# A list for the order of a segment: the recurrent attention half of a two-part kernel, with its evacuations and streamed weights dealt anew

## The chip, the cores and the metric

The kernel runs on one core of one Trainium2 chip. The metric is the device time of one execution in microseconds; three runs of the kernel before gave 1959.92, 1972.41 and 1975.98 us, and their median, 1972.41 us, is the time before. The profile is of one execution of its own.

## The reference

Two independent attentions, their outputs side by side. Part A is a sliding, dilated attention (2048 rows, 32 heads of 20). Part B, which the change is about, is a recurrence over 64 segments of 32 rows, each with 8 memory rows that the segment before has made:

```python
for s in range(n_seg):                                   # 64
    h = jnp.concatenate([mem, xs], axis=1)               # 8 + 32 rows of 640
    q = jnp.einsum('btd,dhe->bhte', h, Wq)               # 32 heads of 192: 640 x 6144 weights
    k, v = ...                                           # the same with Wk, Wv
    scores = jnp.where(mask, q @ k.T * scale, -1e9)
    o = jnp.einsum('bhqk,bhke->bhqe', softmax(scores), v)
    o = jnp.einsum('bhte,hed->btd', o, Wo)               # 6144 x 640
    mem = o[:, :M, :]                                    # feeds the next segment
    outs.append(o[:, M:, :])
```

So each segment needs all four weight matrices (31 MB in bf16), and its memory rows can't be known before the segment before is done.

## The kernel before

Part A runs first, while part B's resident weights are loaded and the others are copied to a DRAM buffer of plain layout (`copy_streamed`, L331). Then `segment` (L677) runs 64 times and `project_late` (L775) makes the remaining output rows.

*Weights.* Each of Wq, Wk, Wv is cut into 4 groups g (8 heads) of 5 pieces dc (128 of the 640 rows, 1536 columns, 384 KB); Wo is cut into 24 pieces of 320 KB, six per group. `STREAMED` (L285) names the pieces that do not fit and are fetched anew in each segment: 8 of k, 10 of v and 6 of o, 24 in all. `get_unit` (L423) gives a piece to the stage that uses it; for a streamed one `fetch` (L418) issues a DMA on SP into a ring of 7 slots (`wstream`). SP takes its DMAs in the program's order, and each waits until its slot's last reader on TensorE (PE) is done.

*Rows.* HX holds the 32 rows `main` that a segment handles itself (8 of memory, 24 of its own) and 32 rows `ahead`: the last 8 rows of four segments, whose projections are made in advance. `RENEW` says which k and v group has its ahead rows projected in a segment (one of each; `project32` then runs 40 matmuls instead of 20); the ahead rows of q are made at the segment's end (`ql`). Between, the late rows wait in buffers Lb, from which POOL copies them into QT and KT (L508); those of v wait in LV[g].

*A segment's stages*, for each of the four groups g:

- q, k: `project_qk` (L521, matmuls L490) into an accumulator (three PSUM banks in rotation); `evacuate` (L524, L497) copies it to `sb` as bf16; `turn` (T, L500, L503) transposes it on PE; `fill_both` (L530, L508) copies the result to QT or KT, which exist once and are overwritten for each group.
- S: `scores` (L551, L558) on PE; `soft_begin` (L563, L565) masks, `soft_exp` (L570) takes the maximum and subtracts it on VectorE and calls Exp on ScalarE, `soft_end` (L576) sums, inverts and writes P on VectorE. t1, which holds the scores, exists once.
- tp: `turn_p` (L591, L595) transposes P on PE; `spread_p` (L599, L601) writes PT on VectorE.
- v: `values` (L543) projects; `keep_values` (L546, L547, L549) copies to Vst on ScalarE, renewed late rows to LV[g] on VectorE. Vst exists once.
- mix (L606, L614) multiplies PT and the values; `keep_mix` (L620, L622) copies the two results to the halves of OT, then POOL copies the late rows out (L623) and stores them (L624).
- out: `project_out` (L634, L642) adds six Wo pieces' products into Y for groups 0 to 2; `project_last` (L657, L664) does group 3.

`turn_x` (L472) brings the next segment's rows from XS into HX once the last projection has read HX, and `load_x` (L468) fetches XS. `join_begin` (L646, ScalarE) and `join_end` (L652, VectorE) add Y's halves; `close` (L667) adds the last projection, transposes the result and writes the memory rows into HX (L672), on which the next segment's first projection waits; POOL stores the output rows (L674).

*Order.* PE, VectorE, ScalarE and SP keep the order in which the program issues their instructions (`manual_schedule`); only POOL's is left to the scheduler. So the text of `segment` is the order on each engine. On PE it reads: q0 k0 q1 Tq0 Tk0 k1 S0 Tq1 Tk1 q2 k2 v0 S1 tp0 Tq2 Tk2 mix0 v1 S2 out0 tp1 q3 k3 mix1 v2 Tq3 Tk3 tp2 out1 (four pairs) S3 out1 (two pairs) mix2 v3 out2 (four) tp3 out2 (two) mix3 ql last, and the turn of ql.

Of the kernel before, what the change touches and what calls it, by code (L numbers as in the profile page):

```python
# [7 lines left out]
FP32 = mybir.dt.float32  # L8
# [15 lines left out]
def part_a(ctx, tc, A_x, A_wqkv, A_wo, out, ident, emit_loads):  # L24
# [241 lines left out]
    with tc.manual_schedule(engines={mybir.EngineType.PE, mybir.EngineType.DVE, mybir.EngineType.Activation}):  # L266
# [4 lines left out]
        for b in range(-1, n_blk):  # L271
# [17 lines left out]
BLOCKS = 18  # L289
LEAD_IN = 114  # L290
HEAD = 5

# [8 lines left out]
def part_b(ctx, tc, B_x, B_mem0, B_Wq, B_Wk, B_Wv, B_Wo, out, ident, n_seg, pre, nbuf, mid):  # L301
# [193 lines left out]
    def to_sb(p, copy):  # L495
        sb = qk_sb.tile([128, 384], BF16, tag="sb", name="sb")
        copy(sb[:], p[:])  # L497
        return sb

    def turn(sb):  # L500
        pt = bank()[:, 0:384].rearrange("p (c j n) -> p c j n", j=4, n=32)
        for c in range(3):
            nc.tensor.matmul(pt[:, c], lhsT=sb[:, 128 * c:128 * c + 128], rhs=ident, start=True, stop=True)  # L503
        return pt
# [22 lines left out]
    def turn_both(s, m, g, sbs):  # L527
        return [turn(sb) for sb in sbs]

    def fill_both(s, m, g, pts, copy):  # L530
# [12 lines left out]
    def values(s, g):  # L543
        return project32([ahead, main] if renewed(s, "v", g) else [main], "v", g)

    def keep_values(g, ps):  # L546
        S_(Vst[:], ps[-1][:])  # L547
        if len(ps) > 1:
            V_(LV[g][:], ps[0][:])  # L549

    def scores(g):  # L551
        Sps = bank()[:, 0:4 * L].rearrange("p (a n) -> p a n", n=L)
        for outer in range(2):
            for a in range(4):
                for h in range(2):
                    k0, k1, c = (0, 128, 2 * h) if outer else (64 * h, 64 * h + 64, 1)
                    at = L * (4 * c + a)
                    nc.tensor.matmul(Sps[64 * h:64 * h + 64, a, :], lhsT=QT[k0:k1, at:at + 64], rhs=KT[k0:k1, c, a, :],  # L558
                                     start=(outer == 0 and a == 0), stop=(outer == 1 and a == 3),
                                     tile_position=(k0, 64 * h))  # L560
        return Sps

    def soft_begin(Sps):  # L563
        t1 = one.tile([128, 4, L], FP32, tag="t1")
        nc.vector.scalar_tensor_tensor(out=t1[:], in0=Sps, scalar=scale,  # L565
                                       in1=mask[:].unsqueeze(1).to_broadcast([128, 4, L]),
                                       op0=ALU.mult, op1=ALU.add)
        return t1

    def soft_exp(t1):  # L570
        mx = small.tile([128, 4], FP32, tag="mx")
        nc.vector.tensor_reduce(out=mx[:], in_=t1[:], axis=AX.X, op=ALU.max)
        nc.vector.tensor_tensor(t1[:], t1[:], mx[:].unsqueeze(2).to_broadcast([128, 4, L]), op=ALU.subtract)  # L573
# [17 lines left out]
    def turn_p(g):  # L591

        pt = bank()[:, 0:256].rearrange("p (l n) -> p l n", l=2)
        for late in range(2):
            nc.tensor.matmul(pt[:, late, :], lhsT=P[:, late].rearrange("p a n -> p (a n)"), rhs=ident,  # L595
                             start=True, stop=True)
        return pt

    def spread_p(pt):  # L599
        PT = one.tile([128, 4, 2, L], BF16, tag="PT")  # L600
        nc.vector.tensor_tensor(PT[:], pt.rearrange("p l (h n) -> p (l h) n", h=2)[:, :, 0:L].unsqueeze(2)  # L601
                                .to_broadcast([128, 4, 2, L]),
                                own[:].unsqueeze(1).unsqueeze(3).to_broadcast([128, 4, 2, L]), op=ALU.mult)
        return PT

# [70 lines left out]

    def segment(s):  # L677
        last = s + 1 == n_seg
        q0 = project_qk(s, "q", 0)
        q0 = evacuate(q0, V_)  # L680
        k0 = project_qk(s, "k", 0)
        if s == 0:
            fetch_first(len(STREAMED["k"][0]))
        k0 = evacuate(k0, S_)
        q1 = project_qk(s, "q", 1)
        q1 = evacuate(q1, S_)
        q0 = turn_both(s, "q", 0, q0)
        fill_both(s, "q", 0, q0, S_)
        k0 = turn_both(s, "k", 0, k0)
        fill_both(s, "k", 0, k0, V_)  # L690
        k1 = project_qk(s, "k", 1)
        k1 = evacuate(k1, S_)
        t0 = soft_begin(scores(0))
        q1 = turn_both(s, "q", 1, q1)
        fill_both(s, "q", 1, q1, S_)
        soft_exp(t0)
        k1 = turn_both(s, "k", 1, k1)
        fill_both(s, "k", 1, k1, S_)
        soft_end(s, 0, t0)
        q2 = project_qk(s, "q", 2)  # L700
        q2 = evacuate(q2, S_)
        k2 = project_qk(s, "k", 2)
        k2 = evacuate(k2, V_)
        v0 = values(s, 0)
        keep_values(0, v0)
        t1 = soft_begin(scores(1))
        PT = spread_p(turn_p(0))
        q2 = turn_both(s, "q", 2, q2)
        fill_both(s, "q", 2, q2, S_)
        k2 = turn_both(s, "k", 2, k2)  # L710
        fill_both(s, "k", 2, k2, S_)
        soft_exp(t1)
        keep_mix(s, 0, mix(0, PT), (S_, S_))
        v1 = values(s, 1)
        keep_values(1, v1)
        if last:
            load_late((0, 1))
        soft_end(s, 1, t1)
        t2 = soft_begin(scores(2))
        Y = ps_y.tile([128, 320], FP32, tag="y")  # L720
        project_out(Y, 0)
        p1 = turn_p(1)
        soft_exp(t2)
        PT = spread_p(p1)
        q3 = project_qk(s, "q", 3)
        q3 = evacuate(q3, S_)
        k3 = project_qk(s, "k", 3)
        if last:
            load_late((2, 3))
        soft_end(s, 2, t2)  # L730
        k3 = evacuate(k3, V_)
        keep_mix(s, 1, mix(1, PT), (S_, V_))
        v2 = values(s, 2)
        keep_values(2, v2)
        load_x(s + 1)
        q3 = turn_both(s, "q", 3, q3)
        fill_both(s, "q", 3, q3, S_)
        k3 = turn_both(s, "k", 3, k3)
        fill_both(s, "k", 3, k3, V_)
        PT = spread_p(turn_p(2))  # L740
        project_out(Y, 1, range(0, 4))
        t3 = soft_begin(scores(3))
        soft_exp(t3)
        project_out(Y, 1, range(4, 6))
        keep_mix(s, 2, mix(2, PT), (S_, V_))
        soft_end(s, 3, t3)
        v3 = values(s, 3)
        keep_values(3, v3)
        if last:
            load_late((4, 5))  # L750
        project_out(Y, 2, range(0, 4))
        PT = spread_p(turn_p(3))
        turn_x(s + 1)
        project_out(Y, 2, range(4, 6))
        part = join_begin(Y)
        keep_mix(s, 3, mix(3, PT), (S_, V_))
        join_end(Y, part)
        if not last:
            gl = (s + 1) % 4
            ql = project32([ahead], "q", gl)  # L760
            sb = to_sb(ql[0], S_)
        Z = bank()[:, 0:160]
        project_last(Z)
        close(s, Z, part)
        if not last:
            pt = turn(sb)
            keep(late_rows(pt, "q", gl, s + 1), "q", gl, S_)
# [63 lines left out]
    def fetch_first(n):  # L831
        for u in first[:n]:
            fetched[u] = fetch(u)
        del first[:n]
# [80 lines left out]
```

## Time and profile before

| | us |
|---|---|
| median of three runs | 1972.41 |
| the profiled execution's own time | 1969.38 |
| its span, first to last instruction | 1967.4 |
| first close of a segment (L672) | 217.1 |
| last one (of 63) | 1875.6 |
| a segment between, mean of 62 | 26.75 |
| granted TensorE clock, mean | 0.995 |

Busy shares of the page run over the whole span, in which part A takes about the first 177 us, segment 0, with all groups renewed and weights still arriving, some 40, and the end some 60. A segment is read from the timeline between one L672 and the next. PE's waits are listed by what ended them; "issue" means that PE waited for nothing that the profile shows. The ring's pieces are called t, and wcopy_k, wcopy_v and wcopy_o are the DRAM copies that they come from.

### The profile page before, as it was taken

What the parts mean: (1) busy time and instruction counts of PE and PEld (TensorE: products, weight loads), DVE (VectorE), ACT (ScalarE), POOL (GpSimd) and SP (SyncE); (2) the same over time, 40 slices, a digit from 0 to 9 for tenths busy, and PEclk for the clock granted to TensorE, in tenths of its full rate; (3) what the DMA queues carried; (4) which work ended last, traced back from release to release, by engine and by line L of the source; (5) the groups of instructions that cost most, each with busy time, mean ns of one, the idle gap of its engine ahead of it and who ended that gap; (6) DMA issues with size and microseconds to landing.
All of it is one profiled execution on the core that took longest, in us unless ns stands there. A gap on an engine that the chain in (4) does not pass through costs nothing.

```text
span 1967.4 us, 95413 instructions
## 1 busy us (share of the span) xinstructions
PE 1782.9 (91%) x41224; PEld 1133.8 (58%) x41224; DVE 1159.7 (59%) x3404; ACT 817.3 (42%) x2287; POOL 573.1 (29%) x1340
## 2 busy tenths in 40 slices
PE   8898999998899989999999899989998998998888
PEld 5565555555555555555555555555555555555558
DVE  4785666565566555666556566656566565656540
ACT  4453444444344444344444444444444444443420
POOL 3000323333323333333333332333332233332220
PEclk9999999999999999999999999999999999999999
DMA  9928999999999999999999999999999999999991
GB/s 330 307 58 302 314 351 351 355 342 348 328 349 346 343 344 359 342 352 357 347 353 344 344 357 345 358 340 347 351 351 342 340 355 349 351 345 337 337 384 49
DMA packets 286370, 649.51 MB, mean 330 GB/s; under 512 B 61140, under 2 KB 76946, under 8 KB 285948
## 3 DMA queue, kind: packets, MB, share of 16 engines
q1 hardware_dynamic: 267036, 630.01, 90.2%
q0 software_dynamic: 18400, 13.08, 2.1%
q8 instruction: 323, 5.29, 1.1%
q14 instruction: 99, 0.81, 0.1%
q10 hardware_dynamic: 512, 0.33, 0.1%
HBM read 629.10 MB, written 23.24 MB: 332 GB/s over the span
## 4 chain that ended last, share of the span: by engine, by line
PE 69%; DMA 15%; DVE 11%; issue 4%; ACT 1%; SPq 1%; ACTq 0%; DVEq 0%
PE acc L490 37%; DMA t<-wcopy_v 9%; PE Y L642 6%; PE px L614 5%; PE px L558 5%; PE px L503 4%; PE pq L95 3%; PE px L664 3%; DVE PT L601 3%; DMA t<-wcopy_k 2%; DMA t<-wcopy_o 2%; PE px L595 2%; PE px L789 1%; PE po L161 1%; DVE t L565 1%
## 5 line engine op out<-in xcount | busy, mean ns | idle before, releaser
L490 PEld LDWEIGHTS <-HX 128*32 128x32 bf16 x19380 | 480.9, 96 | 395.2 <-issue 98.4
L490 PE MATMUL acc<-t,HX 128*32 128x384 bf16 x5816 | 411.4, 328 | 37.7 <-DMA t<-wcopy_v 17.0
L490 PE MATMUL acc<-wres_q,HX 128*32 128x384 bf16 x6460 | 327.8, 328 | 57.8 <-DVE HX L672 47.8
L623 POOL COPY OL<-OT 128x96 bf16<-128x96 bf16 x256 | 157.9, 617 | 549.6 <-ACT OT L622 505.9
L497 ACT CAST sb<-acc 128x384 bf16<-128x384 f32 x383 | 183.9, 480 | 299.2 <-PE acc L490 281.8
L490 PE MATMUL acc<-wres_k,HX 128*32 128x384 bf16 x3880 | 241.1, 327 | 7.5 <-issue 6.7
L497 DVE CAST sb<-acc 128x384 bf16<-128x384 f32 x263 | 143.4, 555 | 165.8 <-PE acc L490 153.0
L508 POOL COPY QT<-Lb 128x96 bf16<-128x96 bf16 x252 | 70.5, 280 | 514.0 <-PE px L558 370.5
L547 ACT CAST Vst<-acc 128x384 bf16<-128x384 f32 x256 | 122.4, 478 | 228.5 <-PE acc L490 227.2
L490 PE MATMUL acc<-wres_v,HX 128*32 128x384 bf16 x3224 | 203.0, 328 | 5.7 <-issue 5.6
L642 PE MATMUL Y<-wres_o,OT 128*32 128x320 bf16 x3584 | 198.5, 301 | 4.0 <-ACT OT L622 2.3
L574 ACT ACTIVATE t<-t 128x160 f32<-128x160 f32 x256 | 87.2, 341 | 238.1 <-DVE t L573 234.0
L503 PE MATMUL px<-ident,sb 128*128 128x128 bf16 x1938 | 165.5, 221 | 3.2 <-issue 1.4
L624 POOL DMA_DIRECT2D late_o<-OL x256 | 139.4, 544 | 81.5 <-POOL OL L623 53.5
L508 DVE CAST KT<-px 128x384 bf16<-128x384 f32 (+1 forms) x161 | 77.0, 494 | 145.7 <-PE px L503 145.2
L614 PE MATMUL px<-PT,Vst 64*128 64x80 bf16 (+1 forms) x2048 | 130.3, 211 | 29.6 <-DVE PT L601 23.3
L558 PEld LDWEIGHTS <-QT 64*64 64x64 bf16 (+1 forms) x4096 | 105.8, 109 | 85.2 <-issue 72.7
L503 PEld LDWEIGHTS <-sb 128*128 128x128 bf16 x1938 | 112.2, 98 | 55.7 <-issue 42.8
L601 DVE TENSOR_TENSOR PT<-px,own 128x320 bf16<-128x320 f32 x256 | 124.0, 484 | 34.5 <-PE px L595 31.5
L508 ACT CAST QT<-px 128x384 bf16<-128x384 f32 (+1 forms) x260 | 123.9, 478 | 46.7 <-PE px L503 46.7
L622 ACT CAST OT<-px 128x240 bf16<-128x240 f32 x320 | 107.4, 359 | 83.2 <-PE px L614 76.0
L565 DVE SCALAR_TENSOR_TENSOR t<-px,mask 128x160 f32<-128x160 f32 x256 | 82.8, 324 | 97.2 <-PE px L558 88.5
(97 smaller groups left out, 2483.0 us busy)
## 6 DMA issues: line engine op xcount, KB each, us to landing
t<-wcopy_v SPq DMA_DIRECT2D x640, 384.0 KB, 5.8
t<-wcopy_k SPq DMA_DIRECT2D x512, 384.0 KB, 5.8
t<-wcopy_o SPq DMA_DIRECT2D x396, 320.0 KB, 5.4
wres_q<-in_B_Wq_dram SPq DMA_DIRECT2D x20, 384.0 KB, 7.8
late_o<-OL POOLq DMA_DIRECT2D x256, 24.0 KB, 5.5
wres_q<-late_o SPq DMA_DIRECT2D x16, 384.0 KB, 7.5
wres_o<-in_B_Wo_dram SPq DMA_DIRECT2D x18, 320.0 KB, 7.2
wres_k<-in_B_Wk_dram SPq DMA_DIRECT2D x12, 384.0 KB, 7.8
```

Of the source, the lines that this page charges most:

```text
L490: nc.tensor.matmul(ps[n][32 * j:32 * j + 32, :], lhsT=X[:, dc, :], rhs=w[:, 384 * j:384 * j + 384], start=(dc == 0), stop=(dc == 4), tile_ ...
L497: copy(sb[:], p[:])
L503: nc.tensor.matmul(pt[:, c], lhsT=sb[:, 128 * c:128 * c + 128], rhs=ident, start=True, stop=True)
L508: copy(t[:, :, :, n0:n1], src)
L547: S_(Vst[:], ps[-1][:])
L558: nc.tensor.matmul(Sps[64 * h:64 * h + 64, a, :], lhsT=QT[k0:k1, at:at + 64], rhs=KT[k0:k1, c, a, :], start=(outer == 0 and a == 0), stop= ...
L601: nc.vector.tensor_tensor(PT[:], pt.rearrange("p l (h n) -> p (l h) n", h=2)[:, :, 0:L].unsqueeze(2) .to_broadcast([128, 4, 2, L]), own[:] ...
L614: nc.tensor.matmul(ps[r][lo:hi, 2 * L * k:2 * L * k + 2 * L], lhsT=V[64 * r:64 * r + 64, col:col + hi - lo], rhs=PT[64 * r:64 * r + 64, 2 ...
L622: copy(OT[:, 6 * r:6 * r + 6].rearrange("p c n -> p (c n)"), ps[r][:, 0:6 * L])
L623: nc.gpsimd.tensor_copy(OL[:, g % 2].rearrange("p n c -> p c n"), OT[:, :, 32:L])
L624: nc.gpsimd.dma_start(late_o[s // 4][:, g, s % 4], OL[:, g % 2].rearrange("p n c -> p (n c)"))
L642: nc.tensor.matmul(Y[t:t + 32].rearrange("p (b c) -> p b c", b=2), lhsT=OT[:, slot(c), 0:32], rhs=wide(w, r, gv), start=(i == 0), stop=(i ...
```

## The change

1. `segment` becomes a reader of a list of tokens: FIRST for segment 0 (the order of before), ORDER for the others. A token stands for a stage's instructions on all engines that it uses: e = evacuate, T = turn and fill, sb / mx / sub / send = the softmax's parts (Exp goes with sub), ve = keep_values, ot = keep_mix, tx = turn_x.
2. EVACUATE, FILL and HEADS name the engine (S ScalarE, V VectorE) of each evacuation (ahead rows, main rows), each fill and each half of OT. Before: main rows of q0, k2, k3 on V and the others on S, all renewed ahead rows on V; fills of k0, k3 on V, the rest on S; OT's halves SS, SV, SV, SV.
3. STREAMED names other pieces, as many of each matrix.
4. `turn_both` and `fill_both` become one function, and `soft_exp` gives its maximum to `soft_max`; `fetch_first`'s second call, in segment 0, is gone.

```diff
-STREAMED = {"q": ((), (), (), ()), "k": ((0, 1, 4), (2, 4), (1,), (2, 3)), "v": ((0, 1, 4), (0, 2, 4), (3,), (0, 3, 4)),
-            "o": (3, 7, 10, 16, 18, 20)}
+STREAMED = {"q": ((), (), (), ()), "k": ((1, 4), (0, 2), (2, 4), (0, 4)), "v": ((1, 2), (0, 4), (2, 3, 4), (0, 2, 4)),
+            "o": (4, 11, 15, 18, 19, 22)}
+ORDER = """
+    q.0 k.0 e.k0 e.q0 T.q0 q.1 T.k0 e.q1 k.1 S.0 T.q1 sb.0 e.k1 k.2 mx.0 sub.0 e.k2 q.2 send.0 T.k1 e.q2
+    v.0 ve.0 S.1 sb.1 T.k2 tp.0 PT.0 T.q2 v.1 mix.0 mx.1 ve.1 sub.1 S.2 k.3 q.3 ot.0 send.1 out.0.0
+    out.0.1 e.q3 e.k3 sb.2 mx.2 sub.2 tp.1 PT.1 T.k3 v.2 T.q3 mix.1 S.3 ot.1 send.2 tp.2 out.1.0 ve.2
+    sb.3 PT.2 mx.3 out.1.1 sub.3 send.3 mix.2 v.3 ot.2 out.2.0 tp.3 tx ve.3 out.2.1 PT.3 mix.3 ot.3 part
+    ql join last eql close Tql
+"""
+EVACUATE = {"k0": "SS", "k1": "SS", "k2": "SS", "k3": "SV", "q0": "SV", "q1": "SS", "q2": "SV", "q3": "SS"}
+FILL = {"k0": "V", "k1": "S", "k2": "S", "k3": "S", "q0": "V", "q1": "S", "q2": "S", "q3": "S"}
+HEADS = ("VS", "SS", "SS", "SV")
...
-    def evacuate(ps, copy):
-        return [to_sb(p, c) for p, c in zip(ps, [V_, copy][2 - len(ps):])]
+    def evacuate(ps, copies):
+        return [to_sb(p, c) for p, c in zip(ps, copies[2 - len(ps):])]
...
     def segment(s):
         last = s + 1 == n_seg
-        q0 = project_qk(s, "q", 0)
-        q0 = evacuate(q0, V_)
-        k0 = project_qk(s, "k", 0)
...
+        def step(name, *at):
+            g = int(at[0][-1]) if at else None
+            if name in "qkv":
+                project(name, g)
+            elif name == "e":
+                m = at[0][0]
+                got["sb", m, g] = evacuate(got.pop((m, g)), [engine[c] for c in EVACUATE[at[0]]])
+            elif name == "T":
+                m = at[0][0]
+                turn_and_fill(s, m, g, got.pop(("sb", m, g)), engine[FILL[at[0]]])
...
+        for token in (ORDER if s else FIRST).split():
+            step(*token.split("."))
```

On PE the list gives, from segment 1 on: q0 k0 Tq0 q1 Tk0 k1 S0 Tq1 k2 q2 Tk1 v0 S1 Tk2 tp0 Tq2 v1 mix0 S2 k3 q3 out0 tp1 Tk3 v2 Tq3 mix1 S3 tp2 out1 mix2 v3 out2 (four) tp3 out2 (two) mix3 ql last, and the turn of ql. All matmuls, copies and DMAs are as many as before.

More of the change, by code (lines that the diff above doesn't have):

```diff
@@ L289 @@
 BLOCKS = 18
+FIRST = """
+    q.0 e.q0 k.0 e.k0 q.1 e.q1 T.q0 T.k0 k.1 e.k1 S.0 sb.0 T.q1 mx.0 sub.0 T.k1 send.0 q.2 e.q2 k.2 e.k2
+    v.0 ve.0 S.1 sb.1 tp.0 PT.0 T.q2 T.k2 mx.1 sub.1 mix.0 ot.0 v.1 ve.1 send.1 S.2 sb.2 out.0.0 out.0.1
+    tp.1 mx.2 sub.2 PT.1 q.3 e.q3 k.3 send.2 e.k3 mix.1 ot.1 v.2 ve.2 T.q3 T.k3 tp.2 PT.2 out.1.0 S.3
+    sb.3 mx.3 sub.3 out.1.1 mix.2 ot.2 send.3 v.3 ve.3 out.2.0 tp.3 PT.3 tx out.2.1 part mix.3 ot.3 join
+    ql eql last close Tql
+"""
[5 more added lines that the diff above has]
+    ql join last eql close Tql
+"""
+EVACUATE = {"k0": "SS", "k1": "SS", "k2": "SS", "k3": "SV", "q0": "SV", "q1": "SS", "q2": "SV", "q3": "SS"}
+FILL = {"k0": "V", "k1": "S", "k2": "S", "k3": "S", "q0": "V", "q1": "S", "q2": "S", "q3": "S"}
+HEADS = ("VS", "SS", "SS", "SV")
 LEAD_IN = 114
@@ L741, in segment @@
[L741 to L767, printed above, removed]
+        engine = {"S": S_, "V": V_}
+        got = {}
+        def project(m, g):
+            if m == "v":
+                got["v", g] = values(s, g)
+            else:
+                got[m, g] = project_qk(s, m, g)
+                if last and (m, g) == ("k", 3):
+                    load_late((2, 3))
@@ new lines, in step @@
+        def step(name, *at):
[8 more added lines that the diff above has]
+                turn_and_fill(s, m, g, got.pop(("sb", m, g)), engine[FILL[at[0]]])
+            elif name == "S":
+                got["S", g] = scores(g)
+            elif name == "sb":
+                got["t", g] = soft_begin(got.pop(("S", g)))
+            elif name == "mx":
+                got["mx", g] = soft_max(got["t", g])
+            elif name == "sub":
+                soft_exp(got["t", g], got.pop(("mx", g)))
+            elif name == "send":
+                soft_end(s, g, got.pop(("t", g)))
+            elif name == "tp":
+                got["p", g] = turn_p(g)
+            elif name == "PT":
+                got["PT", g] = spread_p(got.pop(("p", g)))
+            elif name == "ve":
+                keep_values(g, got.pop(("v", g)))
+                if g == 2:
+                    load_x(s + 1)
+                elif last and g in (1, 3):
+                    load_late((0, 1) if g == 1 else (4, 5))
+            elif name == "mix":
+                got["mix", g] = mix(g, got.pop(("PT", g)))
+            elif name == "ot":
+                keep_mix(s, g, got.pop(("mix", g)), [engine[c] for c in HEADS[g]])
+            elif name == "out":
+                g, half = int(at[0]), int(at[1])
+                if "Y" not in got:
+                    got["Y"] = ps_y.tile([128, 320], FP32, tag="y", name="Y")
+                project_out(got["Y"], g, range(4 * half, 4 + 2 * half))
+            elif name == "part":
+                got["part"] = join_begin(got["Y"])
+            elif name == "join":
+                join_end(got["Y"], got["part"])
+            elif name == "tx":
+                turn_x(s + 1)
+            elif name == "ql":
+                got["ql"] = None if last else project32([ahead], "q", (s + 1) % 4)
+            elif name == "eql":
+                got["sbl"] = None if last else to_sb(got["ql"][0], S_)
+            elif name == "last":
+                got["Z"] = bank()[:, 0:160]
+                project_last(got["Z"])
+            elif name == "close":
+                close(s, got["Z"], got["part"])
+            elif name == "Tql":
+                if not last:
+                    gl = (s + 1) % 4
+                    keep(late_rows(turn(got["sbl"]), "q", gl, s + 1), "q", gl, S_)
```

68 lines of the change are left out of this document (5 added, 63 removed).

## The prediction

> **What bounds the kernel now.** I read the sums by engine and the slices first, then the steady stretch of part B, then what TensorE (PE) waited for, then one segment instruction by instruction.
>
> ```profile
> PE 1782.9 (91%) x41224; PEld 1133.8 (58%) x41224; DVE 1159.7 (59%) x3404; ACT 817.3 (42%) x2287; POOL 573.1 (29%) x1340
> ...
> DMA  9928999999999999999999999999999999999991
> GB/s 330 307 58 302 314 351 351 355 342 348 328 349 346 343 344 359 342 352 357 347 353 344 344 357 345 358 340 347 351 351 342 340 355 349 351 345 337 337 384 49
> ```
>
> Two things are nearly full at once: PE at 91% and the DMA engines at nine tenths in nearly every slice. The steady stretch (first close of a segment to the last, 62 segments of 26.75 us) says it sharper, in its last two columns (DMA share, GB/s):
>
> ```profile
> 217.00:1876.00 1659.00, 1515.94 (x36340) 945.56 (x36343) 999.59 (x3160) 709.47 (x2053) 529.94 (x1242) 1.00 0.98 348
> ```
>
> PE's own waits there:
>
> ```profile
> PE acc L490 <- DVE HX L672: 47.8, 63, 1.0
> PE acc L490 <- issue: 31.0, 37, 2.1
> PE px L614 <- DVE PT L601: 22.4, 99, 0.3
> PE acc L490 <- DMA t<-wcopy_v: 11.7, 26, 1.7
> PE acc L490 <- DVE sb L497: 5.4, 16, 0.3
> ```
>
> The first is the recurrence at a segment's end; it stays. The third is PE waiting for the spread softmax. I laid out the timeline of the 62 whole segments, taking for each stage the time from its first matmul to that of the next stage. Per segment the smallest times add up to 24.41 us, what the medians have more is 1.10 (waits that come every time), what the means have more is 1.24 (weight pieces and instruction fetch, irregular). 24.41 + 1.10 + 1.24 = 26.75. The 1.10 sits in few places: 0.25 and 0.17 before and in mix 0, 0.27 before mix 3, 0.22 between v 3 and output 2 (for OT), small change elsewhere. Another 0.51 comes in each segment with renewed v 0 (k 2's two evacuations both on VectorE), 0.13 on average and inside the 24.41. Three of these in the timeline (start, length; the first three lines are tp 0, PT and mix 0, the fourth is output 2 waiting for OT, the last two PT and mix 3):
>
> ```profile
> 1026.54 0.29 PE L595 MATMUL px<-ident,P 128*128 128x128 bf16 x2
> ...
> 1026.90 0.48 DVE L601 TENSOR_TENSOR PT<-px,own 128x320 bf16<-128x320 f32 x1
> ...
> 1027.43 0.42 PE L614 MATMUL px<-PT,Vst 64*128 64x80 bf16 x4 [0.27 <-DVE PT L601]
> ...
> 1039.16 0.73 PE L642 MATMUL Y<-wres_o,OT 128*32 128x320 bf16 x16 [0.17 <-ACT OT L622]
> ...
> 1040.18 0.49 DVE L601 TENSOR_TENSOR PT<-px,own 128x320 bf16<-128x320 f32 x1 [0.33 <-PE px L595]
> ...
> 1040.72 0.25 PE L614 MATMUL px<-PT,Vst 64*128 64x80 bf16 x4 [0.20 <-DVE PT L601]
> ```
>
> **The change, part by part (us per segment, no renewal unless said).**
>
> *Longer PE order.* Smallest times by what follows: a projection 0.82 before another projection, 0.92 before any other stage; a turn (T) 0.17 before a turn or tp, 0.26 before others; S 0.47, mix 0.44; an output stage of six pairs 0.93, cut in two by a score 0.66 + 0.39. Before, 7 of the 12 projections are followed by another shape, now 9 (+0.20); turns now stand alone seven times (1.67 becomes 1.99, +0.32); tp 1 before a turn saves 0.09, output 1 in one piece 0.12. Sum +0.31. The Trainium skill's "TensorEngine Tiling (Array Packing)", Key Properties, says that changing the tiling mode drains the engine; that speaks against this order, and the 0.92 against 0.82 agrees.
>
> *Waits that go.* Between tp 0 and mix 0 now stand a turn and v 1 (0.26 + 0.92), and PT needs 0.36 to its start, 0.49, 0.05 = 0.90: the 0.25 + 0.17 go. S 3 moves ahead of output 1, so softmax 3's Exp is done before mix 2 ends and OT 2 is copied about 0.2 before output 2 asks: 0.22 goes. q 2 between k 2 and v 0 covers k 2's evacuations: 0.13 goes. Small ones 0.14.
>
> *Waits that come.* T q3 now stands two stages ahead of S 3, which reads it. From a turn's first matmul to its fill's start 0.43 to 0.44, fill 0.48, to PE 0.05:
>
> ```profile
> 1023.07 0.53 PE L503 MATMUL px<-ident,sb 128*128 128x128 bf16 x6
> ...
> 1023.50 0.48 ACT L508 CAST QT<-px 128x384 bf16<-128x384 f32 x1 [0.30 <-PE px L503]
> ```
>
> That is 0.97 against a cover of 0.26 + 0.44: a new wait of 0.27. Behind S 3 everything on PE moves with it. If ScalarE were still at k 3's fill it would be 0.75, if its start were 0.16 earlier, 0.1; k 3's fill starts about 1.2 earlier, so I take 0.27. Mix 3 keeps its wait: tp 3 to PT to mix 3 is 0.90, cover 0.21 + 0.39: 0.30 as now. turn_x now stands before PT 3 on VectorE: 0.38 + 0.18 behind softmax 3's end. It waits for the last v 3 matmul and for XS; if it slipped behind tp 3 it would add up to 0.56. Chain of softmax 3 after S 3 (0.11, four steps of 0.36, 0.35 + 0.21 + 0.39, PT 2 between) ends 0.1 to 0.3 ahead of tp 3, so I take 0. In segments with renewed k 1, q 2 waits 0.24 for an accumulator that ScalarE now empties: 0.06. Others 0.05. Sum 0.68.
>
> *Evacuations.* ScalarE gains about 0.8 (second halves of OT 1 and 2 at 0.36, the renewed k rows at 0.48, less OT 0's first half), VectorE loses as much. ScalarE is busy 709.47 / 62 = 11.4 of 26.75: no price beyond the waits above. join now comes after OT 3 on ScalarE: part (2 x 0.29) and join (2 x 0.31) end 0.2 before the last projection does. Cost nothing as long as that 0.2 holds.
>
> *Queues.* SP issues the same 24 pieces a segment (18 of 384 KB, 6 of 320 KB) in the order of their use; XS still follows v 2's pieces, sixteen pieces in, past the previous segment's stores. POOL does the same copies and stores, each waiting for OT or a score that comes within 1 us of where it was. Segment 0 keeps its order; project_late has other pieces streamed, as many: 0 +-3 us in all.
>
> *Pieces.* With the slots laid end to end, the time from the release of a ring slot to the use of its next piece was 5.5 to 8.8 (shortest: v 3's last piece), and will be 5.0 to 9.0; landing takes 5.8 (part 6 of the page). v 3's 5.5 costs 0.10 on average today, so 5.0 for two pieces (output 2's, the last one of project_last) costs between 0 and 1.6; I take nothing, nearest to that row.
>
> *Sum for PE:* 1.23 of waits go to 0.68, the order is 0.31 longer: -0.24, in 63 segments -15 us.
>
> *How much of it reaches the end.* DMA is at 0.98. Segments by renewal (four kinds) have usual PE sums of 25.41, 25.16, 25.73, 25.59, a spread of 0.57; their mean lengths are 26.81, 26.65, 26.80, 26.74, a spread of 0.16. So transfers even out most of what PE saves. On the other hand slices reach 359 GB/s and one segment took 25.0. Between a quarter and all, I take a half: -0.12 x 63 = -8 us. The profiled execution took 1969.4 (span 1967.4 and 2.0 around it), so 1961.8; the median shown is 3.0 above that execution: **1965**.
>
> **Rivals.**
> *Faster in full:* PE's 0.24 all counts, and the pieces, now mostly in pairs two us apart, take a third off the 1.24 of irregular waits (0.41): 0.65 x 63 = 41, 1931. For it: the best segments have almost no irregular wait. Against: the 0.98. Over 1% from 0.31 a segment.
> *Transfers pace it alone:* no change, 1972 (0.16 of 0.57 says nearly that). The Trainium skill's "DMA: Bandwidth & Descriptors", Bandwidth, gives about 358 GB/s from HBM for a core; an estimate from it for a segment's 348 x 26.75 = 9.3 MB is 26.0 us, which would leave 0.77 at most; the slices of 359 and 384 here are above it.
> *Slower, by the late pieces:* output 2's piece and the last one have 5.0 us from slot to use, against 0.3 for the issue and 5.8 to land. Each would be 1.05 late; with the DMA backlog one pays for part of the other, 1.6 in every second segment: (0.8 - 0.24) x 63 = 35, 2007. It decides from 0.55 a segment. Against: v 3's 5.5 today.
>
> **Chances.** A measurement of this kernel tells about 1% from no change (its three runs span 0.8%). Half of PE's gain 0.40 (1965, own range 1950 to 1980, 0.03 of it over 1% faster); in full 0.26; no change 0.11; late pieces 0.23. Faster 0.26 + 0.03 = 0.29, slower 0.23, the rest 0.48. A third of each outer case left out (0.09 + 0.08) gives 1925 to 2012.
>
> **What would show it.** PE waiting for PT about 0.3 x 63 instead of 99 waits, all at mix 3; no wait for OT at output 2; a new wait of S 3 (L573 of the changed kernel) for ScalarE's fill, some 0.27 x 63 = 17 us, put down to PE's weight load; DMA share 0.98 or more at about 350 GB/s; segments of about 26.6. I am wrong if PE's waits for t in output 2 or project_last exceed 0.5 a segment, if PT 3 stands behind turn_x, or if the DMA share falls below 0.97 with the time.

## The result, and the profile after

| | before | after |
|---|---|---|
| median of 11 runs each, same chip, us | 1975.98 | 1952.96 |
| their range | 1959.92 to 1981.97 | 1946.30 to 1960.26 |
| ratio, 95% interval | | 0.9889 (0.9864 to 0.9915) |
| the profiled execution, us | 1969.38 | 1954.89 |
| segment, mean of 62 | 26.75 | 26.55 |

1.1% faster, 22 us by the ratio and 23 by the medians; between the two profiled executions it is 14.5 us, since the one of before lay in the lower half of its runs. Of the 14.3 us between the two spans, 12.6 lie in the 62 segments, 0.5 before them and 1.2 behind them. So 0.20 us a segment by the profiles, about 0.35 by the ratio of all runs (22 / 63).

The page of the changed kernel, sums by engine and the last two rows of the slices:

```profile
PE 1786.8 (91%) x41224; PEld 1129.4 (58%) x41224; DVE 1094.8 (56%) x3206; ACT 870.7 (45%) x2485; POOL 571.0 (29%) x1340
...
DMA  9928899999999999999999999999999999999991
GB/s 329 311 59 292 309 343 349 351 350 361 340 354 353 329 352 352 353 363 338 361 363 344 332 350 347 353 343 338 357 345 352 355 347 362 354 353 354 357 385 60
```

VectorE gave 65 us, ScalarE took 53. The steady stretch, last columns clock, DMA share and GB/s:

```profile
217.00:1862.00 1645.00, 1518.20 (x36332) 939.59 (x36324) 938.79 (x2972) 757.24 (x2231) 526.29 (x1240) 0.99 0.98 350
```

PE is busy as long as before (1518 against 1516) in a stretch that is 14 us shorter: what went is idle time. A segment moves 350 x 26.55 = 9.3 MB, as before. PE's waits in that stretch:

```profile
PE acc L507 <- DVE HX L690: 47.5, 62, 0.9
PE px L632 <- DVE PT L619: 13.8, 59, 0.8
PE px L573 <- ACT QT L525: 13.6, 62, 0.5
PE acc L507 <- issue: 10.5, 20, 1.5
PE Y L660 <- issue: 8.5, 9, 1.9
PE acc L507 <- DMA t<-wcopy_v: 8.4, 20, 1.1
PE px L632 <- issue: 7.0, 7, 1.8
PE px L682 <- DMA t<-wcopy_o: 3.7, 6, 1.2
...
PE Y L660 <- DMA t<-wcopy_o: 2.5, 4, 1.4
```

The wait for PT comes 59 times and no longer 99: mix 0's is gone, mix 3's stays. S 3 (L573) waits once a segment for T q3's fill, 0.21 as the view counts it. The waits for VectorE's evacuations (5.4 us before) are gone. One segment of PE's timeline (start, length) shows T q3, the first line of mix 1, S 3, and then the first two lines of mix 3:

```profile
1028.69 0.34 PE L520 MATMUL px<-ident,sb 128*128 128x128 bf16 x3
1028.96 0.24 PE L632 MATMUL px<-PT,Vst 64*128 64x80 bf16 x4
...
1029.69 0.54 PE L573 MATMUL px<-KT,QT 64*64 64x40 bf16 x16 [0.21 <-ACT QT L525]
...
1034.09 0.23 PE L632 MATMUL px<-PT,Vst 64*128 64x80 bf16 x3 [0.20 <-DVE PT L619]
1035.81 0.21 PE L632 MATMUL px<-PT,Vst 64*128 64x80 bf16 x1 [1.49 <-issue]
```

From T q3's first matmul to S 3's it is 1.00; the fill in ScalarE's timeline starts 0.38 after T q3's first matmul and takes 0.48:

```profile
1029.07 0.48 ACT L525 CAST QT<-px 128x384 bf16<-128x384 f32 x1 [0.38 <-PE px L520]
```

The last PE line is another kind of stall: 1.49 us in the middle of a mix, between two matmuls of the same form on the same operands. VectorE's timeline shows turn_x (two lines) ahead of PT 3, and that it did not hold it: tp 3 starts at 1033.22, PT 3 0.33 later, the usual distance (median 0.32). In 13 of the 62 segments PT 3 starts 0.42 to 0.54 after tp 3, all of them with renewed v 3: there it stands behind the copy of v 3's late rows on VectorE, which costs 0.03 on average.

```profile
1032.99 0.36 DVE L483 STREAM_TRANSPOSE HX<-XS 128x160 bf16<-128x160 bf16 x1
1033.38 0.17 DVE L494 COPY HX<-HX 128x40 bf16<-128x40 bf16 x1
1033.55 0.49 DVE L619 TENSOR_TENSOR PT<-px,own 128x320 bf16<-128x320 f32 x1
```

**A table for all kernels.** Every step from one matmul's start to the next is sorted by where it falls. At the *first matmul of a stage* lie the waits for other engines, the shape changes and the recurrence. At *pieces*: the first matmuls on a streamed piece, what they take beyond the same place of a kernel that streams nothing (experiment 5 below). *Inside*: all other matmuls, likewise less that kernel's. What is left, 17.09 in the new order and 16.96 in the old one (which has one stage boundary more), is PE's own pace inside stages. Microseconds per segment, from the profiled executions:

| kernel | own | first of stage | pieces | inside | segment |
|---|---|---|---|---|---|
| before | 16.96 | 7.89 | 0.53 | 1.37 | 26.75 |
| after | 17.09 | 7.96 | 0.52 | 0.98 | 26.55 |
| 1, after with the old pieces | 17.09 | 8.02 | 0.76 | 0.92 | 26.79 |
| 2, after with the old order | 16.96 | 8.38 | 0.67 | 1.19 | 27.20 |
| 3, after with the old engines | 17.09 | 8.90 | 0.51 | 0.79 | 27.28 |
| 6, before with the new pieces | 16.96 | 7.89 | 1.10 | 1.15 | 27.10 |
| 10, before with the new engines | 16.96 | 8.39 | 0.29 | 1.26 | 26.91 |
| 11, before with the new order | 17.09 | 8.81 | 0.84 | 1.07 | 27.82 |
| 4, after, no Wo pieces | 17.09 | 7.96 | -0.02 | 0.91 | 25.94 |
| 5, after, no pieces at all | 17.09 | 7.99 | 0.00 | 0.09 | 25.17 |
| 7, after, T q3 early | 17.09 | 7.54 | 0.97 | 1.10 | 26.70 |
| 8, 7 with ql split | 16.92 | 7.63 | 0.94 | 1.00 | 26.49 |
| 9, 8 with other pieces | 16.92 | 7.64 | 0.53 | 1.26 | 26.36 |

In the old order, about 0.22 of "inside" and 0.13 of "pieces" are waits for other engines that fall there (mix 0's second part, two of 0.04, and v 0's accumulator).

### The profile page after: what moved, and what is told of

The parts are those of the page before. It is cut to its first block, busy times and chain, and to the rows that moved or that the text cites. A ratio compares the mean times of both kernels' runs of the same rounds, so it can differ in the third digit from the quotient of the medians.

```text
span 1953.1 us, 95447 instructions
## 1 busy us (share of the span) xinstructions
PE 1786.8 (91%) x41224; PEld 1129.4 (58%) x41224; DVE 1094.8 (56%) x3206; ACT 870.7 (45%) x2485; POOL 571.0 (29%) x1340
## 4 chain that ended last, share of the span: by engine, by line
PE 71%; DMA 14%; DVE 8%; issue 3%; ACT 2%; SPq 0%; ACTq 0%; POOL 0%; POOLq 0%; DVEq 0%
PE acc L507 40%; DMA t<-wcopy_o 8%; PE px L520 6%; PE px L573 5%; PE Y L660 4%; DMA t<-wcopy_v 4%; PE px L632 3%; PE pq L95 3%; PE px L682 3%; PE px L613 2%; DVE PT L619 1%; PE px L790 1%; PE po L161 1%; DVE Vst L483 1%; DVE XS L687 1%
## 5 line engine op out<-in xcount | busy, mean ns | idle before, releaser
L507 PEld LDWEIGHTS <-HX 128*32 128x32 bf16 x19380 | 468.1, 96 | 358.6 <-DVE HX L690 59.5
L514 ACT CAST sb<-acc 128x384 bf16<-128x384 f32 x454 | 211.2, 480 | 304.9 <-PE acc L507 293.9
L520 PE MATMUL px<-ident,sb 128*128 128x128 bf16 x1938 | 205.6, 222 | 4.0 <-issue 2.7
L660 PE MATMUL Y<-wres_o,OT 128*32 128x320 bf16 x3840 | 188.4, 301 | 8.5 <-issue 7.3
L640 ACT CAST OT<-px 128x240 bf16<-128x240 f32 x384 | 125.0, 359 | 114.5 <-PE px L632 112.4
L525 ACT CAST QT<-px 128x384 bf16<-128x384 f32 (+1 forms) x195 | 93.4, 481 | 164.5 <-PE px L520 164.5
L514 DVE CAST sb<-acc 128x384 bf16<-128x384 f32 x192 | 106.5, 555 | 102.1 <-PE acc L507 86.8
L660 PEld LDWEIGHTS <-OT 128*32 128x32 bf16 x4608 | 116.3, 96 | 65.6 <-issue 19.7
L573 PE MATMUL px<-KT,QT 64*64 64x40 bf16 (+1 forms) x4096 | 138.3, 189 | 14.3 <-ACT QT L525 13.9
L573 PEld LDWEIGHTS <-QT 64*64 64x64 bf16 (+1 forms) x4096 | 108.0, 109 | 70.4 <-issue 61.8
L632 PE MATMUL px<-PT,Vst 64*128 64x80 bf16 (+1 forms) x2048 | 122.5, 212 | 18.0 <-DVE PT L619 14.2
```

The source lines that it names most:

```text
L507: nc.tensor.matmul(ps[n][32 * j:32 * j + 32, :], lhsT=X[:, dc, :], rhs=w[:, 384 * j:384 * j + 384], start=(dc == 0), stop=(dc == 4), tile_ ...
L525: copy(t[:, :, :, n0:n1], src)
L632: nc.tensor.matmul(ps[r][lo:hi, 2 * L * k:2 * L * k + 2 * L], lhsT=V[64 * r:64 * r + 64, col:col + hi - lo], rhs=PT[64 * r:64 * r + 64, 2 ...
L640: copy(OT[:, 6 * r:6 * r + 6].rearrange("p c n -> p (c n)"), ps[r][:, 0:6 * L])
L660: nc.tensor.matmul(Y[t:t + 32].rearrange("p (b c) -> p b c", b=2), lhsT=OT[:, slot(c), 0:32], rhs=wide(w, r, gv), start=(i == 0), stop=(i ...
```

## The experiments

Ratios are to the kernel before in the same comparison, with their 95% intervals. PE's waits of experiments 1, 5, 6, 7 and 12 are taken from 217 to 1850 us of the span, and those of 10 to 1885; the steady stretches end between 1773 (5) and 1899 (6). One theory was that the new order carries the gain and that the engines and the pieces are there to serve it; the rivals were that one of the parts alone makes it, or that the transfers set the time whatever the order.

### One part taken back: 1, 2, 3

**1**, the pieces:

```diff
-STREAMED = {"q": ((), (), (), ()), "k": ((1, 4), (0, 2), (2, 4), (0, 4)), "v": ((1, 2), (0, 4), (2, 3, 4), (0, 2, 4)),
-            "o": (4, 11, 15, 18, 19, 22)}
+STREAMED = {"q": ((), (), (), ()), "k": ((0, 1, 4), (2, 4), (1,), (2, 3)), "v": ((0, 1, 4), (0, 2, 4), (3,), (0, 3, 4)),
+            "o": (3, 7, 10, 16, 18, 20)}
```

> The changed kernel with the streamed pieces of before. If the order on TensorE made the gain (theory), the time stays at the changed kernel's, ratio to before 0.985 to 0.993 (about 1953 us against 1976). If the new pieces made it (rival), at least half is given back: ratio 0.994 or more.

Measured: 1981.16 us, ratio 1.0048 (1.0015 to 1.0082): the gain is gone, as the rival said. Its waits for pieces:

```profile
PE acc L507 <- DMA t<-wcopy_k: 20.4, 39, 1.5
...
PE acc L507 <- DMA t<-wcopy_v: 10.1, 24, 0.8
```

After has 0.3 us of the first. k 3 now runs before q 3 and 4.0 us after the release of its piece's slot (the usual stage times laid end to end, release of the slot's last reader to first use), where landing takes 5.5 to 5.8 us from issue (part 6 of the page). Not renewed, the stage takes 1.22 in the median and not 0.82; the mean cost at k 3's pieces is 0.39, at v 1's 0.19. The order of after with the pieces of before would not have been faster.

**2**, the order (segments 1 to 63 run in FIRST as segment 0 does):

```diff
-        for token in (ORDER if s else FIRST).split():
+        for token in FIRST.split():
```

> The changed kernel with the list of segment 0 (the order of before) for all segments; new engines for the evacuations and new pieces stay. Theory: TensorE's usual waits come back to about 25.5 us a segment and the ratio to 0.996 to 1.004. Rival (engines or pieces made the gain): ratio below 0.992.

Measured: 1997.44 us, 1.0123 (1.0076 to 1.0170), above the 0.996 to 1.004 of the theory. In the table it has 0.42 more than after at the first matmuls of stages, 0.15 more at pieces and 0.21 more inside.

**3**, the engines:

```diff
-EVACUATE = {"k0": "SS", "k1": "SS", "k2": "SS", "k3": "SV", "q0": "SV", "q1": "SS", "q2": "SV", "q3": "SS"}
-FILL = {"k0": "V", "k1": "S", "k2": "S", "k3": "S", "q0": "V", "q1": "S", "q2": "S", "q3": "S"}
-HEADS = ("VS", "SS", "SS", "SV")
+EVACUATE = {"k0": "VS", "k1": "VS", "k2": "VV", "k3": "VV", "q0": "VV", "q1": "VS", "q2": "VS", "q3": "VS"}
+FILL = {"k0": "V", "k1": "S", "k2": "S", "k3": "V", "q0": "S", "q1": "S", "q2": "S", "q3": "S"}
+HEADS = ("SS", "SV", "SV", "SV")
```

> The changed kernel with the evacuations, fills and halves of OT on the engines of before. Theory (the order made the gain, the engines only keep its covers): TensorE's usual waits rise by 0 to 0.3 us a segment, ratio 0.987 to 0.997. Rival (the engines made the gain): ratio 0.997 or more.

Measured: 2004.92 us, 1.0173 (1.0129 to 1.0218), far outside the 0.987 to 0.997 of the theory. More than all of what it loses against after lies in the first matmuls of stages (8.90 against 7.96 us a segment). One segment of its VectorE, and then of its PE (S 3 and tp 2), shows the larger half:

```profile
1025.53 0.41 DVE L640 CAST OT<-px 128x240 bf16<-128x240 f32 x1 [0.96 <-PE px L632]
1025.86 0.31 DVE L596 TENSOR_REDUCE sm<-t 128x4 f32<-128x160 f32 x1
1026.20 0.18 DVE L597 RECIPROCAL sm<-sm 128x4 f32<-128x4 f32 x1
1026.41 0.58 DVE L606 TENSOR_TENSOR P<-t,sm 128x128 bf16<-128x128 f32 x2
```

```profile
1025.60 0.54 PE L573 MATMUL px<-KT,QT 64*64 64x40 bf16 x16 [0.21 <-ACT QT L525]
1026.89 0.40 PE L613 MATMUL px<-ident,P 128*128 128x128 bf16 x2 [0.75 <-DVE P L606]
```

The list issues ot.1 ahead of send.2. With OT 1's second half on VectorE, VectorE stands 0.96 waiting for mix 1, and softmax 2's sum, reciprocal and P stand behind it although they are ready; tp 2 then waits 0.75 here, and in 61 of the 62 segments (42.3 us in all). HEADS "SS" for group 1 takes that copy off VectorE; that is what the token order needs from the table of engines. Another loss is renewed k 0 with the turn that follows, 0.27 on average: both evacuations of the old deal end later, and T q0 waits for VectorE's `sb`. A third is output 2, which waits 11.7 us in all for the half of OT that VectorE copies.

### One part alone: 6, 10, 11

Each is the kernel before with one of the three. 10 has the new EVACUATE, FILL and HEADS: it is after with the edits of 1 and 2 together. 11 has the new ORDER: it is after with the edits of 1 and 3 together. 6 has the new STREAMED:

```diff
-STREAMED = {"q": ((), (), (), ()), "k": ((0, 1, 4), (2, 4), (1,), (2, 3)), "v": ((0, 1, 4), (0, 2, 4), (3,), (0, 3, 4)),
-            "o": (3, 7, 10, 16, 18, 20)}
+STREAMED = {"q": ((), (), (), ()), "k": ((1, 4), (0, 2), (2, 4), (0, 4)), "v": ((1, 2), (0, 4), (2, 3, 4), (0, 2, 4)),
+            "o": (4, 11, 15, 18, 19, 22)}
```

> The kernel before with nothing changed but the streamed pieces. Theory now (the pieces are fitted to the order, since the changed kernel with the old ones lost all its gain): no gain or a loss, ratio 0.999 to 1.012, with TensorE waiting for v 2's three pieces. Rival (the new pieces are better in any order): ratio 0.993 or less.

> The kernel before with the new engines for evacuations, fills and halves of OT alone (old order, old pieces). With the new pieces as well it was at 1.012, of which some 0.013 is what the new pieces alone cost in the old order. Theory (engines are fitted to the order too): usual times 25.6 to 25.9, ratio 1.000 to 1.008. Rival (the new engines are better by themselves): ratio 0.996 or less.

> The kernel before with the new order alone (old engines, old pieces). With new pieces it was at 1.017, by waits for evacuations (k 0 when renewed, S 3, OT 2: usual times 26.5). The old pieces come 4.0 us after their slots in k 3 in this order. Theory: usual times 26.4 to 26.9, ratio 1.015 to 1.035. Rival (old pieces suit the old engines' slower pace): ratio under 1.010.

Measured: 6, 1993.88 us, 1.0129 (1.0089 to 1.0168); 10, 1979.56 us, 1.0056 (1.0025 to 1.0087); 11, 2032.80 us, 1.0327 (1.0285 to 1.0369). None of the three gains alone, and no two of them do (1 is order with engines, 2 engines with pieces, 3 order with pieces). With before and after these are all eight combinations, and only all three parts together gain. What each lacks can be read from the waits. Kernel 6:

```profile
PE acc L490 <- DMA t<-wcopy_v: 30.8, 48, 2.2
...
PE Y L642 <- DMA t<-wcopy_o: 9.6, 13, 1.4
PE px L664 <- DMA t<-wcopy_o: 5.2, 11, 1.3
```

45.6 us for v and o pieces to 1850 us, against 14.7 in before's whole steady stretch: the pieces are spaced for another order. Kernel 10:

```profile
PE px L632 <- DVE PT L619: 22.9, 101, 0.3
...
PE px L573 <- ACT KT L525: 15.3, 58, 0.8
```

A score waits for k 3's fill, now on ScalarE, in 58 segments, and mix 0's wait for PT is still there. Kernel 11 has both faults of 1 and 3 (in its whole steady stretch 28.7 us for k pieces and 38.6 us of tp 2 for P).

### No weight traffic: 4, 5

Both are after with resident weights in place of streamed ones, so that this part of the computation is changed: in 4 the six Wo pieces, in 5 all 24. All matmuls stay.

The edit of 4, in get_unit (STAND_IN names a resident piece of the same group for each of the six):

```diff
+        if STAND_IN and u[0] == "o" and streamed(u):
+            return res["o", STAND_IN[u[1]], 0]
```

and that of 5 (stand_in gives the group's first resident piece):

```diff
+        if streamed(u):
+            return stand_in(u)
```

> The changed kernel without the six streamed Wo pieces: a resident piece stands in for each, so 18 pieces a segment are fetched instead of 24 and those products are of other weights; the matmuls are as many. Theory (transfers near their limit keep back part of what TensorE saves, 1.48 us of irregular waits a segment): DMA share falls to about 0.8, the irregular waits to under 0.5, the segment to about 25.4 us, some 65 us less: ratio 0.95 to 0.965. Rival (the irregular waits are instruction fetch and do not depend on the weights' traffic): segment 26.2 or more, ratio 0.98 or more.

> The changed kernel without any streamed piece: in segments a resident piece of the same matrix and group stands in for each of the 24, so the products are partly of other weights and the ring is idle; matmuls and instructions are as many. Without 6 of them TensorE still waited 0.43 us a segment for nothing that the profile shows (instruction fetch, by the spacing of about 128 matmuls), and 0.02 for pieces. Theory (those fetches are late because the DMA engines are busy with weights): irregular waits under 0.25, segment 25.1 to 25.3, ratio to before 0.945 to 0.953. Rival (they are late whatever the traffic): irregular waits 0.7 or more, segment 25.7 or more, ratio 0.963 or more.

Measured: 4, 1907.70 us, 0.9672 (0.9621 to 0.9723), DMA share 0.83. It is slower than I expected, 25.94 a segment and not 25.4: the waits for pieces fell to nearly nothing, but the stalls inside stages stayed (0.91 against 0.98). 5, 1858.09 us, 0.9444 (0.9415 to 0.9474). Its steady stretch, and all of PE's waits from 217 us to 1850 (the last two lines lie behind the stretch):

```profile
213.00:1773.00 1560.00, 1479.72 (x36332) 925.47 (x36332) 936.49 (x2972) 756.33 (x2231) 525.66 (x1240) 1.00 0.04 10
```

```profile
PE acc L513 <- DVE HX L696: 49.4, 62, 1.1
PE px L638 <- DVE PT L625: 15.6, 63, 0.4
PE px L579 <- ACT QT L531: 13.3, 62, 0.2
PE px L638 <- issue: 0.6, 1, 0.6
PE px L688 <- ACT OT L646: 0.5, 1, 0.5
```

Three waits are left in a segment: the recurrence, mix 3's, S 3's. So the new order's own pace on PE is 25.17, and 1.38 of after's 26.55 come from the weight traffic, the waits put down to "issue" (29 us in after's steady stretch, none in this one) among them.

### Less PE time: 7, 8, 9, 12

**7** takes away S 3's wait by turning q 3 one stage earlier, ahead of v 2; **8** also does the first of ql's five steps ahead of mix 3, to cover its wait; **9** also picks the pieces anew, so that the shortest time from a slot's release to its use is 5.46 us and no longer 4.33 (after: 4.77).

In all three:

```diff
-    out.0.1 e.q3 e.k3 sb.2 mx.2 sub.2 tp.1 PT.1 T.k3 v.2 T.q3 mix.1 S.3 ot.1 send.2 tp.2 out.1.0 ve.2
+    out.0.1 e.q3 e.k3 sb.2 mx.2 sub.2 tp.1 PT.1 T.k3 T.q3 v.2 mix.1 S.3 ot.1 send.2 tp.2 out.1.0 ve.2
```

In 8 and 9 also (the step ql then takes a part of its five steps; that code is left out here):

```diff
-    sb.3 PT.2 mx.3 out.1.1 sub.3 send.3 mix.2 v.3 ot.2 out.2.0 tp.3 tx ve.3 out.2.1 PT.3 mix.3 ot.3 part
-    ql join last eql close Tql
+    sb.3 PT.2 mx.3 out.1.1 sub.3 send.3 mix.2 v.3 ot.2 out.2.0 tp.3 tx ve.3 out.2.1 ql.0 PT.3 mix.3 ot.3 part
+    ql.1 join last eql close Tql
```

In 9 also:

```diff
-STREAMED = {"q": ((), (), (), ()), "k": ((1, 4), (0, 2), (2, 4), (0, 4)), "v": ((1, 2), (0, 4), (2, 3, 4), (0, 2, 4)),
-            "o": (4, 11, 15, 18, 19, 22)}
+STREAMED = {"q": ((), (), (), ()), "k": ((0, 1, 3), (0, 1), (0, 3), (0, 4)), "v": ((1, 3, 4), (4,), (0, 3, 4), (1, 4)),
+            "o": (0, 11, 16, 17, 20, 23)}
```

> The changed kernel with the turn of q 3 right after that of k 3, ahead of v 2: the fill that S 3 waits for (0.29 us a segment) gets v 2's 0.92 as cover, and one shape switch (0.08) goes. Theory (a saving on TensorE that comes in every segment reaches the end by about a half): usual times fall by 0.37, the segment by 0.15 to 0.25, ratio to before 0.977 to 0.985. Rival (transfers and fetches pace it): segment within 0.05 of the changed kernel's, ratio 0.986 to 0.991. Rival (all of it comes through): ratio 0.977 or less.

> The same, and the first of ql's five steps (0.17 us) stands between the last part of output 2 and mix 3, so that PT 3 is nearer to done when mix 3 asks (it waits 0.26 us there); OT 3's copies keep 0.66 as cover. Theory (half comes through): another 0.05 to 0.1 us a segment, ratio 0.002 to 0.003 below the run with the turn alone. Rivals: nothing (paced by transfers), or a loss, if the pieces of project_last now come too early for their slots.

> The run with the early turn of q 3 and the split ql, with other streamed pieces (as many of each matrix), picked so that the shortest time from a ring slot's release to the use of its next piece, on the usual stage times laid end to end, is 5.5 us; it is 4.3 with the pieces of the changed kernel, which have regular waits there (v 3, output 2, project_last). Theory (what the two shorter covers saved was lost to pieces that came too early for their slots): the regular waits in v 3 and output 2 go, usual times fall to about 24.7, the segment to 26.0 to 26.3, ratio to before 0.972 to 0.984. Rival (the average transfer rate paces the segment, whatever the spacing): segment within 0.1 of 26.5, ratio 0.986 or more.

Measured: 7, 1956.19 us, 0.9916 (0.9891 to 0.9941); 8, 1947.69 us, 0.9896 (0.9855 to 0.9937); 9, 1947.53 us, 0.9902 (0.9869 to 0.9935). The intervals hold after's ratio: none of them can be told from it, though each takes PE waits away. For 7 the expected 0.977 to 0.985 was missed. The table says where the time went. 7 saves 0.42 at the first matmuls of stages and pays 0.45 at the pieces. Its waits:

```profile
PE acc L507 <- DMA t<-wcopy_v: 18.3, 42, 1.4
...
PE px L682 <- DMA t<-wcopy_o: 8.9, 21, 1.8
...
PE Y L660 <- DMA t<-wcopy_o: 4.9, 9, 1.2
```

32.1 us (to 1850 us) where after has 14.6, with S 3's wait gone: v 3 (1.03 in the median, 0.82 in after) and output 2 (0.89, 0.75) now ask for their pieces sooner than the slots allow. 9 mends that (pieces back to 0.53, though 0.26 of it is now at v 0, whose pieces are not those with the shortest time) with own and first of stage together at 24.56 against after's 25.05, but then the stalls inside stages are 0.28 more. The steady stretch of 9:

```profile
217.00:1852.00 1635.00, 1505.45 (x36335) 929.50 (x36336) 938.82 (x2975) 754.33 (x2236) 531.43 (x1241) 1.00 0.99 353
```

I had expected 0.972 to 0.984 of it and missed.

**12** asks how much the transfers leave when PE is far ahead. It leaves out steps dc 1 to 3 of every q projection, 60 of about 586 matmuls of a segment (this part of the sum is not computed), and keeps every transfer.

```diff
-        for dc in range(5)[part]:
+        for dc in (0, 4) if m == "q" else range(5)[part]:
```

> The changed kernel with three of the five steps of each q projection left out (4 groups and ql, 60 matmuls a segment, all of resident weights); all transfers stay. TensorE's usual times fall by 5 x 3/5 x 0.82 = 2.46 us to 22.6 a segment. Theory (the transfers have a pace of their own, near 26 us a segment, and the changed kernel is close to it): the segment falls by no more than 0.7, to 25.8 to 26.5, DMA share 0.99 or more, ratio to before 0.965 to 0.987. Rival (half of what TensorE saves still comes through): 25.3 or less, ratio 0.948 or less.

Measured: 1892.90 us, 0.9645 (0.9583 to 0.9707), segment 25.34:

```profile
218.00:1789.00 1571.00, 1406.23 (x32612) 842.74 (x32612) 936.58 (x2975) 754.26 (x2237) 526.79 (x1241) 0.99 1.00 367
```

PE's pace fell by 60 x 0.041 = 2.46, the segment by 1.21. The line of v pieces in PE's waits, and the rate in slices of 47 us:

```profile
PE acc L507 <- DMA t<-wcopy_v: 46.0, 91, 2.0
```

```profile
GB/s 326 326 74 221 314 374 367 372 374 377 359 377 372 375 358 347 370 368 348 369 363 368 375 352 371 374 357 361 385 365 367 364 376 371 355 376 364 367 374 45
```

The DMA share is 1.00 and PE now stands for pieces, so the transfers hold it up here; but the slots are still released by PE, and single slices reach 385. So 25.3 is the most that the transfers need in a segment, not a measured floor. It is below the 26 that I had expected, and within 0.2 of PE's own 25.17. By the time alone the rival fits about as well: 1.21 of 2.46 is a half, and it asked for 25.3 or less. What speaks against a fixed half are experiments 7 to 9.

## Why the prediction was right, and where not

The time, 1952.96, lies 12 us below the forecast of 1965 and inside the range. The forecast was a gain of 8 us from 1972.41; measured were 22 from 1975.98. "Faster" had the smaller chance (0.29) than "same" (0.48), and it came out at the border between the two.

*PE's sum, -0.24.* It held. By position (own, first of stage, and the engine waits inside: 0.22 + 0.13 before, none after) PE goes from 25.20 to 25.05, -0.15. Counted by medians of stages, as the prediction did, and with the regular waits at pieces taken out, it goes from 25.42 to 25.09, -0.33 (25.51 less 0.09 at v 3's piece; 25.07 less 0.09 at output 2's piece, and 0.11 more for two waits that come in one kind of segment only, below). The forecast lies between the two counts. Its terms:

- S 3's new wait: 0.27 forecast; S 3 with mix 1 is longer by 0.29. The place and the cause are right. That the size is right is luck: the fill starts 0.38 after the turn and not 0.43, but S 3 starts 0.14 after the fill's end (1029.55 to 1029.69 in the lines above, and in the median) and not 0.05, and the two nearly cancel. Why it is 0.14 is not shown.
- Mix 3's wait stays: forecast as before plus 0.03, measured 0.03 less. The turns, with the wait ahead of mix 0: forecast +0.07 (0.32 - 0.25), measured +0.05. Output 1 and the tp stages: -0.21 and some small waits, measured -0.26. All right.
- Accumulators: q 2 in segments with renewed k 1 waits 0.20 (forecast 0.24). Not forecast: q 1 waits 0.22 in those with renewed k 0. Each is 0.05 on average.
- "7 of the 12 projections are followed by another shape, now 9 (+0.20)" was wrong: it is still 7. q 3 and v 3 end in an output stage, and those take 0.81 and 0.82. Both have the tile form 128\*32 (the profile's lines), so nothing changes. The 0.92 of v 3 in before was a wait for OT that never fell below 0.1. I had counted by the name of the stage. The Trainium skill's "TensorEngine Tiling (Array Packing)", Key Properties, says it the right way: changing the *mode* drains the engine, not going to another tile. The same slip hid 0.10 of mix 0, which now stands before S 2 (64\*64 behind 64\*64: 0.34, not 0.44).
- OT's wait at output 2 goes, but only 0.13 of the 0.22 was that wait; the rest stood at v 3's piece. These misses nearly cancel.

*Evacuations at no price:* right for the kernel as changed; VectorE's and ScalarE's other work hides them. Experiments 3, 10 and 11 show that this holds only together with the order: the same order with the old deal costs 0.94 a segment, the new deal in the old order 0.50. The join's margin of 0.2 did not hold: VectorE's half of it ends 0.09 before the close in the median (0.73 in before). The close then starts 0.08 after the last matmul where it was 0.05, so the price was only some 0.02.

*"I take nothing" for the pieces:* about right in size, within its 0 to 1.6. Pieces cost 0.53 before (0.13 of it the accumulator) and 0.52 after, so +0.12. The places are those named: output 2's piece 0.14, the last stage's 0.10; and v 2 and v 3, which I had not named. Shortest time from slot to use is 4.77, forecast 5.0. The rival of late pieces (0.8 a segment) did not come; experiments 1 and 6 show it where pieces and order do not fit. Its sum took 5.8 us to land, the row of the k and v pieces; both pieces that it named are of Wo, whose row has 5.4 in before.

*"I take a half":* this is the step that was mis-sized, on weak grounds. By the profiles 0.20 of 0.15 to 0.33 reached the end, by the ratio of all runs about 0.35; so most of it or all. The argument was that transfers at a DMA share of 0.98 even out what PE saves. Its row, mean lengths that differ by 0.16 where usual sums differ by 0.57, did not show that: each mean is of 15 or 16 segments that spread by 0.79, so its standard error (the scatter to expect of such a mean) is 0.15 to 0.25. Experiment 12 shows that 0.98 was not full: with PE ahead the same bytes flow in 25.3 a segment. Experiments 7 to 9 show the other side: 0.4 to 0.5 more off PE brought nothing that can be measured, by the pieces' slots (7, 8) or by more stalls inside stages (9). No fixed share describes both.

*The rival "transfers alone pace it"* (no change, 0.11) and with it the estimate of 26.0 from the Trainium skill's "DMA: Bandwidth & Descriptors", Bandwidth, fall with experiment 12: 367 GB/s over 1571 us is above the 358 it was worked out from. The Trainium skill's "HBM Reference", Specifications (TRN2), says that 358 is each core's share when both of a pair stream and that one alone gets more; the trace agrees as far as 367.

*What remains open.* Inside stages the stalls fell from 1.15 (1.37 less the engine waits) to 0.98, which is 0.17 of the net 0.20. Across the other kernels that stream all 24 pieces they lie between 0.79 and 1.26 in one profiled execution each, and I can name no edit that sets them, so this part may be chance. Counted as waits for "issue" of over 0.15 us, they are 40 in after and 50 in before, a difference no larger than the chance scatter of such counts (the root of 90 is 9). So what of the gain between the two profiles is the order's, and what is fewer stalls in one execution, stays open. It was not tried whether the kernel before without streaming has 25.2 or 25.4 of its own pace, which would settle PE's sum.

In one picture: PE alone needs 25.17, the transfers alone at most 25.3. Coupled by seven slots, they take 26.55. No change tried here gained without both fewer waits on PE and pieces that fall where the order can use them, and after is the only one of the eight combinations in which both fit.

## What to carry to other kernels

Where two resources are nearly full, measure each one's own pace by taking the other away (no streaming; less compute at all the transfers) before reasoning about what share of a gain comes through. When an order of stages changes, work out anew for each prefetched piece the time from its slot's release to its use, and for each in-order engine which copy stands ahead of which chain; here each of order, engines and pieces cost 0.6 to 3.3% without the other two. And count a shape change by the tile form in the profile's line, not by the stage's name.

## What the runs showed of the hardware that I had not expected

A DMA share of 0.98 at 350 GB/s was no ceiling: experiment 12 ran 1.00 at 367, and a slice of its page, well inside the steady stretch, reached 385.

Stalls between matmuls with nothing to wait for (up to 1.9 us, 29 us a run) come and go with the weight traffic: 0.98 a segment in after, 0.09 in experiment 5. They are PE's instructions arriving late through the same DMA engines. Part 3 of the pages lists that queue, after's first and then experiment 12's:

```profile
q8 instruction: 323, 5.29, 1.1%
```

```profile
q8 instruction: 293, 4.80, 1.0%
```

Experiment 12 has 3876 matmuls fewer (41224 against 37348 on the pages), and as many weight loads, and 30 packets less: some 258 instructions and 16 KB to each. So the queue carries them. No view ties a stall to a packet, but the trace has every packet's start and length, and they do: each of the 40 waits for "issue" in after's steady stretch ends 1.24 to 1.62 us after the end of a packet of this queue. In before 49 of 50 end within 1.20 to 1.65 us behind one, in experiment 12 all 20. A moment taken at random lies so in 7 to 8% of the cases, and PE's other waits in after do so in 18 of 218. Experiment 5 moves as many packets (323) without such waits, so it takes the weight traffic to make them late.
